# Part of w_out's rows moved from SyncE's queue to four-engine GpSimd loads, in a one-token decode kernel

## The chip, the cores and the metric

The kernel runs on one core of a Trainium2 chip. The metric is the device time in microseconds of one execution. Each time of a kernel is a median of several runs; a profile is one execution of its own, whose time is given beside its span.

## The reference

One token x (576 values) is normalized, and two branches are computed from it and added to it. Branch A is attention with a cache: 32 query heads, 16 key and value heads, of which the last 4096 positions are used. Branch B is a gated MLP with 2304 inner values.

```python
xn = layernorm(x)                                   # (1, 1, 576)
# A: attention over the last 4096 positions
q = (xn @ wq).reshape(32 heads, 128)
k, v = k_cache[:, :, -4096:], v_cache[:, :, -4096:] # 16 heads, each for two query heads
o = softmax(q @ k.T * 128 ** -0.5) @ v
A = o.reshape(4096) @ wo                            # wo: (4096, 576)
# B: gated MLP
z = gelu(xn @ w_in)                                 # w_in: (576, 4608)
z1, z2 = z[:2304], layernorm(z[2304:])
g = w_sp * z2 + b_sp                                # w_sp and b_sp are one value each
B = (z1 * g) @ w_out                                # w_out: (2304, 576)
out = x + A + B
```

Everything is bfloat16 in HBM. The two caches are 16.8 MB each as far as they are used, wq 4.7 MB, w_in 5.3 MB, wo 4.7 MB and w_out 2.7 MB.

## The kernel before

**Loads.** All large loads are issued by SyncE in the order of the list `order` (lines 103 to 104), w_out after it (line 117). They write tiles of one pool with eight buffers (`units`, line 60), so SyncE waits, before an issue, until PE has finished with the tile eight places before it. The order is wq (in parts), k0 to k3, v0, v1, two parts of w_in, and then k, v, the rest of w_in and wo in turn; the last ones are v6, v7, wo3 and w_out. Here k0 stands for the keys of two heads, 2 MB in 128 rows of 16 KB, one to a partition; v0 likewise. `wout_v` (line 78) puts 18 consecutive rows of w_out on each partition, and line 117 loads them in four pieces of 8, 6, 3 and 1 rows. ScalarE issues three tiny loads: x (line 71) and the two values w_sp and b_sp (lines 387, 388). GpSimd issues no load.

**Tables.** At the start GpSimd makes the identity and then `row_of` (lines 146 to 151), a table of 18 matrices of 128 x 128 ones and zeros. DVE makes small tables from the identity, among them `rem` and `col_of` (lines 152 to 153 and 209 to 216). With the two, `z_gate` (line 350) and `z_rows` (line 365) bring the gated values, which lie with the index 128 c + p, to the layout that w_out's rows have, 18 p + r: `z_gate` multiplies them into `spread`, and 18 matmuls with `row_of` as weights give `hp`, which DVE copies to `hv`, a column for each of a partition's 18 rows.

**Attention.** Blocks of the keys are transposed by eight matmuls (`T`, line 225) into PSUM, copied to a kT buffer by DVE or ScalarE (a pool of 20, `KTB`, line 35), and multiplied with q (`S`, line 237). The loop of line 404 runs over three rounds j = 1 to 3. In each, sixteen blocks of T run ahead of S by five, and of the products with v of the round before (`PV`, line 283) by seven. Between the rounds stand the softmax steps (`sm_max`, `sm_tr`, `sm_exp`, `sm_rec`), and the parts of the list in line 403: w_in's products (`z_part`), a permutation of the attention's output (`O_perm`) and the products with wo (`WO`). The gelu follows the third part of w_in; `z_gate` and `z_rows` are in round 3, at c = 1 and 8. PE's instructions run in the order in which they are written.

**The end.** After the last round come the PV of the last two pairs of heads (v6 and v7), `O_perm(3)`, `WO(3)`, and w_out's 18 rows (line 443). Each row is four matmuls of 144 columns, side by side in four column groups of the array (`out_mm`, line 305), all adding into one PSUM tile, `out_ps`. DVE copies it, and SyncE stores it.

## Time and profile before

| | |
|---|---|
| median of 3 runs | 130.89 us (130.76 to 131.17) |
| the profiled execution | 130.86 us, span 129.1 us |
| mean granted TensorE clock in it | 0.762 |
| bytes read | 50.96 MB, 395 GB/s over the span |
| PE, DVE, ScalarE, GpSimd busy | 72%, 45%, 22%, 6% of the span |
| w_out: first and last issue, last landing | 105.28, 110.72 and 125.69 us |
| PE's last matmul ends, the store is issued | 126.01, 126.40 us |

All times in the profile are microseconds from the start of the span. PE is TensorE, PEld its weight loads, DVE VectorE, ACT ScalarE, POOL GpSimd, SP SyncE; a q after a name means the engine's issuing side. In the chain of work, each line has its start, its length and what it was, a DMA from its issue to its landing; a timeline's lines have start, busy time, engine, line of the code, operation, output, inputs and shapes, and in brackets the idle time before it and what ended it. "Issue" stands there for a wait that no event in the profile explains. A digit in the rows of slices is the busy share of one fortieth of the span in tenths; q1 is SyncE's queue, q10 ScalarE's, and q8 the fetching of instructions.

### The profile page before, as it was taken

To read this page: it belongs to the slowest core of one execution; us is meant where nothing else is said; L and a number is where in the kernel's file an instruction comes from. 1 tells how busy PE (TensorE), PEld (TensorE's weight loads), DVE (VectorE), ACT (ScalarE), POOL (GpSimd) and SP (SyncE) were. 2 spreads that over 40 slices of the span, in tenths; PEclk is the share of its full clock that TensorE was granted. 3 is DMA by queue.
4 is the path that set the end of the run, shared out by engine and by line. 5 is a ranking of instruction groups with operands and counts; after the bars stand their busy time and mean duration, and the time that the engine had idled before them with its cause. 6 is when DMAs were issued, how large, how long until landed. Compare 5 with 4: busy or idle time off the path is not lost.

```text
span 129.1 us, 4567 instructions
## 1 busy us (share of the span) xinstructions
PE 93.1 (72%) x2135; PEld 86.9 (67%) x2135; DVE 57.8 (45%) x146; ACT 29.0 (22%) x34; POOL 7.1 (6%) x9
## 2 busy tenths in 40 slices
PE   3013999883986997927998959479549999587480
PEld 3013988773975997827988958468439998477460
DVE  6976768400564444305464524484823333430100
ACT  3001174500134353001363330105233330100000
POOL 7940000000000000000000000000000000000000
PEclk9999999965577699855599995558997555555559
DMA  4999999999999999999999999999999999999830
GB/s 117 436 398 444 436 426 402 448 431 416 416 431 431 413 428 416 439 416 436 411 431 421 424 396 449 416 436 421 426 426 411 415 433 431 419 407 416 358 135 0
DMA packets 4495, 51.23 MB, mean 397 GB/s; under 512 B 509, under 2 KB 638, under 8 KB 1022
## 3 DMA queue, kind: packets, MB, share of 16 engines
q1 hardware_dynamic: 4472, 50.96, 94.0%
q8 instruction: 16, 0.26, 0.8%
q14 instruction: 1, 0.01, 0.0%
q10 hardware_dynamic: 6, 0.00, 0.0%
HBM read 50.96 MB, written 0.00 MB: 395 GB/s over the span
## 4 chain that ended last, share of the span: by engine, by line
DMA 51%; PE 35%; issue 5%; DVE 4%; SPq 2%; ACT 1%
DMA v<-in_A_v_cache_dram 22%; DMA wq<-in_A_wq_dram 16%; PE tp L230 16%; DMA wout<-in_B_w_out_dram 13%; PE s L245 8%; PE o L289 5%; PE q_ps L377 2%; SPq L86 2%; PE zp L323 1%; DVE d L268 1%; DVE ss L273 1%; ACT p L270 1%; PE su L278 1%; PE s L242 1%; DVE mx L250 1%
## 5 line engine op out<-in xcount | busy, mean ns | idle before, releaser
L230 PE MATMUL tp<-ident,k 128*128 128x128 bf16 x512 | 44.5, 250 | 3.0 <-DVE kT L234 1.8
L230 PEld LDWEIGHTS <-k 128*128 128x128 bf16 x512 | 37.1, 114 | 4.2 <-issue 2.8
L234 DVE COPY kT<-tp 128x1024 bf16<-128x1024 bf16 x40 | 27.3, 690 | 24.5 <-PE tp L230 24.1
L232 ACT COPY kT<-tp 128x1024 bf16<-128x1024 bf16 x24 | 24.2, 1012 | 47.4 <-PE tp L230 47.4
L289 PE MATMUL o<-p,v 128*128 128x4 bf16 x512 | 19.8, 165 | 5.6 <-issue 2.9
L245 PE MATMUL s<-q_bf,kT 128*128 128x4 bf16 x512 | 20.9, 166 | 3.3 <-issue 3.3
L245 PEld LDWEIGHTS <-kT 128*128 128x128 bf16 x512 | 18.8, 102 | 4.3 <-issue 4.3
L289 PEld LDWEIGHTS <-v 128*128 128x128 bf16 x512 | 16.7, 100 | 6.3 <-issue 3.6
L250 DVE TENSOR_REDUCE mx<-s 128x8 f32<-128x512 f32 x4 | 2.8, 692 | 13.5 <-PE s L245 13.5
L270 ACT ACTIVATE p<-d 128x512 bf16<-128x512 f32 x4 | 2.5, 629 | 25.5 <-DVE d L268 25.5
L377 PEld LDWEIGHTS <-wq 128*128 128x128 bf16 x144 | 4.1, 101 | 2.7 <-issue 2.2
L377 PE MATMUL q_ps<-xe,wq 128*128 128x2 bf16 x144 | 4.0, 164 | 2.5 <-DVE xe L196 2.2
L278 PE MATMUL su<-ss,ones_f 128*128 128x8 f32 x8 | 2.2, 345 | 4.7 <-DVE ss L273 4.7
L278 PEld LDWEIGHTS su<-ss,ones_f 128*128 128x128 f32 x8 | 1.8, 279 | 5.2 <-DVE ss L273 5.2
L292 DVE TENSOR_TENSOR oTn<-o,rm 128x4 bf16<-128x4 f32 x8 | 1.3, 162 | 8.2 <-PE o L289 8.2
L307 PE MATMUL out_ps<-wo,oP 128*1 128x144 bf16 x128 | 4.5, 320 | 0.6 <-DVE oP L303 0.6
L323 PEld LDWEIGHTS <-win 128*128 128x128 bf16 x162 | 4.7, 104 | 0.1
L323 PE MATMUL zp<-xe,win 128*128 128x2 bf16 x162 | 4.8, 165 | 0.0
L168 PE MATMUL x_ps<-x,twice 64*128 64x9 bf16 x1 | 0.2, 164 | 5.3 <-DVE x L166 5.3
L273 DVE TENSOR_REDUCE ss<-p 128x8 f32<-128x512 bf16 x4 | 2.7, 686 | 2.8 <-ACT p L270 2.8
L264 PE MATMUL bc<-dg,ones_f 8*128 8x8 f32 x8 | 2.3, 360 | 2.3 <-issue 2.3
L307 PEld LDWEIGHTS <-oP 128*1 128x1 bf16 x128 | 3.3, 115 | 0.9 <-DVE oP L303 0.7
(94 smaller groups left out, 55.5 us busy)
## 6 DMA issues: line engine op xcount, KB each, us to landing
v<-in_A_v_cache_dram SPq DMA_DIRECT2D x8, 2048.0 KB, 27.3
k<-in_A_k_cache_dram SPq DMA_DIRECT2D x7, 2048.0 KB, 26.7
win<-in_B_w_in_dram SPq DMA_DIRECT2D x3, 1728.0 KB, 28.0
wo<-in_A_wo_dram SPq DMA_DIRECT2D x4, 1152.0 KB, 27.6
wq<-in_A_wq_dram SPq DMA_DIRECT2D x2, 2048.0 KB, 14.1
k<-in_A_k_cache_dram SPq DMA_DIRECT2D x2, 1024.0 KB, 11.1
wout<-in_B_w_out_dram SPq DMA_DIRECT2D x1, 1152.0 KB, 16.8
wout<-in_B_w_out_dram SPq DMA_DIRECT2D x1, 864.0 KB
```

Source lines behind the costliest of these rows:

```text
L230: nc.tensor.transpose(tp[:, i, :], kn[b][:, 8 * c + i, :], ident[:])
L232: nc.scalar.copy(kT[n][:], tp[:])
L234: nc.vector.tensor_copy(kT[n][:], tp[:])
L245: nc.tensor.matmul(s_ps[j][:, i, 8 * c + t, :], lhsT=kT[n][:, t, :], rhs=q_bf[:, 4 * b:4 * b + 4], start=False, stop=True, skip_group_chec ...
L250: nc.vector.tensor_reduce(out=mx[:], in_=s_ps[j][:].rearrange("p i t c -> p i c t"), axis=AXX, op=ALU.max)
L270: nc.scalar.activation(p[:], d[:], ACT.Exp, scale=SCALE)
L273: nc.vector.tensor_reduce(out=ss[:], in_=p[:].rearrange("p i t c -> p i c t"), axis=AXX, op=ALU.add)
L278: nc.tensor.matmul(su[:], lhsT=ones_f[:], rhs=sm[j]["ss"][:].rearrange("p i c -> p (i c)"), start=True, stop=True)
L289: nc.tensor.matmul(sm[j]["o"][:], lhsT=vn[b][:, t, :], rhs=p_sb[j][:, i, t, :], start=t == 0, stop=t == NT - 1)
L307: nc.tensor.matmul(out_ps[32 * g:32 * g + 1, :], lhsT=lhsT, rhs=rhs[:, OW * g:OW * (g + 1)], start=start, stop=last, tile_position=(0, 32 ...
L323: nc.tensor.matmul(zp[:, c, :], lhsT=win_t[r][:, P * c:P * (c + 1)], rhs=xe_of(r), start=(r == rows.start and c == 0), stop=r == rows.stop ...
L377: nc.tensor.matmul(q_ps[:, c, :], lhsT=wq_t[r][:, P * c:P * (c + 1)], rhs=xe_of(r), start=(r == 0 and c == 0), stop=r == NS - 1, skip_grou ...
```

## The change

w_out's first 1792 rows stay on SyncE's queue, 14 to a partition, in pieces of 7, 4, 2 and 1 rows. The other 512 go, eight to a partition, to 64 partitions: 16 to 31, 48 to 63, 80 to 95 and 112 to 127. They are a tile `wx` of their own, zero on the other partitions, and are loaded by four GpSimd DMAs of 16 partitions each (`load_wx`), in whose access pattern the source's outermost dimension has four elements and the destination's 16. Ahead of each stands a load of one value to each of four partitions of `junk4`. Two memsets on DVE, written after `z_part(2)` and `sm_rec(1)` at the end of round 1, touch `wx` and `junk4` first, so the loads wait for them. The eight rows of `wx` are multiplied between `WO(3)` and the rest of w_out, so the end has 22 rows of four matmuls. The tables follow the two layouts: `row_of` is made for 14 matrices of the first kind and four of the second, with more and smaller steps on GpSimd, which also sets `wx` to zero; `colA` and `colB` take the place of `col_of`, and `spreadB` stands beside `spread`. To make room, `KTB` goes from 20 to 16.

```diff
+RA = 14
+RB = 8
+FA = RA * P
+CB = FR - RA
-KTB = 20
+KTB = 16
...
-    wout_v = B_w_out.rearrange("(p r) n -> p r n", r=FR)
+    wout_v = B_w_out[0:FA].rearrange("(p r) n -> p r n", r=RA)
...
-    load_rows(wout_t, wout_v, "wout", D, (0, 8, 14, 17, 18))
+    load_rows(wout_t, wout_v, "wout", D, (0, 7, 11, 13, 14))
...
+    wx = const.tile([P, RB * D], BF16, name="wx")
+    wx_v = B_w_out[FA:FH].rearrange("(b s e r) n -> b e s (r n)", b=CB, s=4, r=RB)
+    junk4 = const.tile([4, 2], BF16, name="junk4")
...
-    nc.gpsimd.memset(row_of[:], 1.0)
-    nc.gpsimd.affine_select(out=row_of[:], in_=row_of[:], compare_op=ALU.is_ge, fill=0.0, base=0,
-                            pattern=[[P, FR], [-FR, P]], channel_multiplier=1)
+    nc.gpsimd.memset(row_of[:], 0.0)
+    nc.gpsimd.memset(row_of[:, 0:RA, :], 1.0)
+    nc.gpsimd.affine_select(out=row_of[:, 0:RA, :], in_=row_of[:, 0:RA, :], compare_op=ALU.is_ge, fill=0.0, base=0,
+                            pattern=[[P, RA], [-RA, P]], channel_multiplier=1)
...
+    for b in range(CB):
+        to = row_of[:, RA + b, 32 * b + 16:32 * b + 32].rearrange("m (e s) -> m e s", s=4)
+        nc.gpsimd.memset(to, 1.0)
+        nc.gpsimd.affine_select(out=to, in_=to, compare_op=ALU.is_ge, fill=0.0, base=0,
+                                pattern=[[-RB, 4], [-4 * RB, 4]], channel_multiplier=1)
+        nc.gpsimd.affine_select(out=to, in_=to, compare_op=ALU.is_ge, fill=0.0, base=RB - 1,
+                                pattern=[[RB, 4], [4 * RB, 4]], channel_multiplier=-1)
+    nc.gpsimd.memset(wx[:], 0.0)
...
-        spread = const.tile([P, FR, FR], BF16, name="spread")
-        nc.vector.tensor_tensor(out=spread[:], in0=col_of[:], in1=g[:].unsqueeze(2).to_broadcast([P, FR, FR]), op=ALU.mult)
-        return spread
+        spread = const.tile([P, RA, RA], BF16, name="spread")
+        nc.vector.tensor_tensor(out=spread[:], in0=colA[:], in1=g[:, 0:RA].unsqueeze(2).to_broadcast([P, RA, RA]), op=ALU.mult)
+        spreadB = const.tile([P, CB, RB], BF16, name="spreadB")
+        nc.vector.tensor_tensor(out=spreadB[:], in0=colB[:].unsqueeze(1).to_broadcast([P, CB, RB]),
+                                in1=g[:, RA:FR].unsqueeze(2).to_broadcast([P, CB, RB]), op=ALU.mult)
+        return spread, spreadB
...
+    def load_wx():
+        nc.vector.memset(wx[:, 0:1], 0.0)
+        nc.vector.memset(junk4[:], 0.0)
+        for b in (0, 2, 1, 3):
+            nc.gpsimd.dma_start(junk4[:, 0:1], B_w_out[FA:FA + 4, 0:1])
+            nc.gpsimd.dma_start(wx[32 * b + 16:32 * b + 32, :], wx_v[b])
...
+            if what == "z2":
+                load_wx()
...
-    for j in range(FR):
-        out_mm(hv[:, j:j + 1], wout_t[j], last=j == FR - 1)
+    for r in range(RB):
+        out_mm(hv[:, RA + r:RA + r + 1], wx[:, D * r:D * (r + 1)])
+    for j in range(RA):
+        out_mm(hv[:, j:j + 1], wout_t[j], last=j == RA - 1)
```

More of the change, by code (lines that the diff above doesn't have):

```diff
@@ L143 @@
     selr = const.tile([P, 8, 8, 16], BF16, name="selr")
+    wx = const.tile([P, RB * D], BF16, name="wx")
+    wx_v = B_w_out[FA:FH].rearrange("(b s e r) n -> b e s (r n)", b=CB, s=4, r=RB)
+    junk4 = const.tile([4, 2], BF16, name="junk4")
     row_of = const.tile([P, FR, P], BF16, name="row_of")
-    nc.gpsimd.memset(row_of[:], 1.0)
-    nc.gpsimd.affine_select(out=row_of[:], in_=row_of[:], compare_op=ALU.is_ge, fill=0.0, base=0,
-                            pattern=[[P, FR], [-FR, P]], channel_multiplier=1)
-    nc.gpsimd.affine_select(out=row_of[:], in_=row_of[:], compare_op=ALU.is_ge, fill=0.0, base=FR - 1,
-                            pattern=[[-P, FR], [FR, P]], channel_multiplier=-1)
-    rem = const.tile([P, 2, FR], FP32, name="rem")
-    col_of = const.tile([P, FR, FR], BF16, name="col_of")
+    nc.gpsimd.memset(row_of[:], 0.0)
+    nc.gpsimd.memset(row_of[:, 0:RA, :], 1.0)
+    nc.gpsimd.affine_select(out=row_of[:, 0:RA, :], in_=row_of[:, 0:RA, :], compare_op=ALU.is_ge, fill=0.0, base=0,
+                            pattern=[[P, RA], [-RA, P]], channel_multiplier=1)
+    nc.gpsimd.affine_select(out=row_of[:, 0:RA, :], in_=row_of[:, 0:RA, :], compare_op=ALU.is_ge, fill=0.0, base=RA - 1,
+                            pattern=[[-P, RA], [RA, P]], channel_multiplier=-1)
+    for b in range(CB):
[6 more added lines that the diff above has]
+    nc.gpsimd.memset(wx[:], 0.0)
+    remA = const.tile([P, 2, RA], FP32, name="remA")
+    colA = const.tile([P, RA, RA], BF16, name="colA")
+    colB = const.tile([P, RB], FP32, name="colB")
     out_ps = ps_c.tile([P, OW], FP32, name="out_ps")
@@ L208 @@
     nc.vector.tensor_copy(selr[:], ident[:].rearrange("p (q r) -> p r q", r=8).unsqueeze(2).to_broadcast([P, 8, 8, 16]))
-    whole = P // FR * FR
-    nc.vector.tensor_reduce(out=rem[:, 0, :], in_=ident_f[:, 0:whole].rearrange("p (q k) -> p k q", k=FR), axis=AXX, op=ALU.add)
-    nc.vector.tensor_add(rem[:, 0, 0:P - whole], rem[:, 0, 0:P - whole], ident_f[:, whole:P])
-    nc.vector.tensor_copy(rem[:, 1, :], rem[:, 0, :])
-    rem_r = rem[:].rearrange("p a k -> p (a k)")
-    for c in range(FR // 2):
-        nc.vector.tensor_copy(col_of[:].rearrange("p (b c) r -> p c b r", b=2)[:, c],
-                              rem_r[:, FR - 2 * c:2 * FR - 2 * c].unsqueeze(1).to_broadcast([P, 2, FR]))
+    whole = P // RA * RA
+    nc.vector.tensor_reduce(out=remA[:, 0, :], in_=ident_f[:, 0:whole].rearrange("p (q k) -> p k q", k=RA), axis=AXX, op=ALU.add)
+    nc.vector.tensor_add(remA[:, 0, 0:P - whole], remA[:, 0, 0:P - whole], ident_f[:, whole:P])
+    nc.vector.tensor_copy(remA[:, 1, :], remA[:, 0, :])
+    nc.vector.tensor_reduce(out=colB[:], in_=ident_f[:].rearrange("p (q k) -> p k q", k=RB), axis=AXX, op=ALU.add)
+    remA_r = remA[:].rearrange("p a k -> p (a k)")
+    for c in range(RA // 2):
+        nc.vector.tensor_copy(colA[:].rearrange("p (b c) r -> p c b r", b=2)[:, c],
+                              remA_r[:, RA - 2 * c:2 * RA - 2 * c].unsqueeze(1).to_broadcast([P, 2, RA]))
     kT, s_ps, p_sb, sm = {}, {}, {}, {}
@@ L312, in WO @@
             out_mm(oP[:, j, r:r + 1], wo_t[j][:, D * r:D * (r + 1)])
-    hv = const.tile([P, FR], BF16, name="hv")
+    hv = const.tile([P, RA + RB], BF16, name="hv")
     zacc = const.tile([P, FR, 2], FP32, name="zacc")
@@ L360, in z_gate, with z_rows @@
         nc.vector.tensor_mul(g[:], G[:, 0, :], gz[:])
-        spread = const.tile([P, FR, FR], BF16, name="spread")
-        nc.vector.tensor_tensor(out=spread[:], in0=col_of[:], in1=g[:].unsqueeze(2).to_broadcast([P, FR, FR]), op=ALU.mult)
-        return spread
-    def z_rows(spread):
-        hp = ps_m.tile([P, FR], FP32, name="hp", tag="m")
+        spread = const.tile([P, RA, RA], BF16, name="spread")
[4 more added lines that the diff above has]
+        return spread, spreadB
+    def z_rows(spread, spreadB):
+        hp = ps_m.tile([P, RA + RB], FP32, name="hp", tag="m")
         for c in range(FR):
-            nc.tensor.matmul(hp[:], lhsT=row_of[:, c, :], rhs=spread[:, c, :], start=c == 0, stop=c == FR - 1)
+            lo, hi, w = (0, RA, spread[:, c, :]) if c < RA else (RA, RA + RB, spreadB[:, c - RA, :])
+            nc.tensor.matmul(hp[:, lo:hi], lhsT=row_of[:, c, :], rhs=w, start=c in (0, RA), stop=c in (RA - 1, FR - 1))
         nc.vector.tensor_copy(hv[:], hp[:])
+    def load_wx():
[4 more added lines that the diff above has]
+            nc.gpsimd.dma_start(wx[32 * b + 16:32 * b + 32, :], wx_v[b])
     q_ps = ps_m.tile([P, 16, 2], FP32, name="q_ps", tag="m")
@@ L416 @@
             if j == 3 and c == 1:
-                spread = z_gate(G, sz)
+                spread, spreadB = z_gate(G, sz)
             if j == 3 and c == 8:
-                z_rows(spread)
+                z_rows(spread, spreadB)
             if c == ROUND + SLAG - 1:
```

## Prediction

> **What bounds the kernel now.** I read the shares of the engines first, then the chain that ended last in order of time, then PE's timeline of the last 35 us. From the page:

> ```profile
> PE 93.1 (72%) x2135; PEld 86.9 (67%) x2135; DVE 57.8 (45%) x146; ACT 29.0 (22%) x34; POOL 7.1 (6%) x9
> DMA  4999999999999999999999999999999999999830
> q1 hardware_dynamic: 4472, 50.96, 94.0%
> q8 instruction: 16, 0.26, 0.8%
> ```

> SyncE's queue (q1) keeps all sixteen DMA engines full until the last tenth of the span, so one expects the end to be set by bytes. The chain in order of time says where that is so:

> ```profile
> 67.50 28.78 DMA v<-in_A_v_cache_dram
> 96.33 0.35 PE o L289 x8
> ...
> 108.45 0.65 PE o L289 x24
> 109.12 16.20 DMA wout<-in_B_w_out_dram
> 125.36 0.69 PE out_ps L307 x16
> 126.07 0.31 DVE res L447
> ```

> The reader is to see two meetings of PE with the DMA engines: v4, issued at 67.50, lands at 96.28 and restarts PE at 96.33; and w_out's third piece restarts it at 125.36. Between them PE works or waits for itself:

> ```profile
> 96.33 0.35 PE L289 MATMUL o<-p,v 128*128 128x4 bf16 x8 [1.87 <-DMA v<-in_A_v_cache_dram]
> ...
> 120.31 0.38 PE L289 MATMUL o<-p,v 128*128 128x4 bf16 x8 [1.42 <-issue]
> 120.94 0.35 PE L298 MATMUL op<-oTn,selr 128*128 128x8 bf16 x8 [0.25 <-DVE oTn L292]
> 121.87 1.13 PE L307 MATMUL out_ps<-wo,oP 128*1 128x144 bf16 x32 [0.57 <-DVE oP L303]
> 122.78 1.18 PE L307 MATMUL out_ps<-wout,hv 128*1 128x144 bf16 x32
> 124.30 0.89 PE L307 MATMUL out_ps<-wout,hv 128*1 128x144 bf16 x24 [0.34 <-DMA wout<-in_B_w_out_dram]
> 125.36 0.65 PE L307 MATMUL out_ps<-wout,hv 128*1 128x144 bf16 x16 [0.17 <-DMA wout<-in_B_w_out_dram]
> ```

> From 122.78 the eighteen rows of w_out would need 18 x 0.12 us (the matmul groups of a row start 0.12 us apart here); the first group of the last row starts at 125.73 instead of 124.82, so waiting for w_out costs 0.91 us in all. That is the whole of what a faster w_out can give, however early it lands.

> The trace keeps sixteen landings of each load, one per DMA engine. They are even early (k1: 17.5 to 18.0, with one at 19.5) and split later: v4's come at 92.8 to 93.1 (seven), 93.7 (one), 94.4 to 94.7 (five) and 96.1 to 96.3 (three); w_out's last row lands at 122.3 to 123.1 (eight), 124.3 (one) and 125.4 to 125.7 (seven). The step is 1.5 us, and a new engine falls back just after each packet of q8. These packets (16 KB, 1.02 to 1.10 us, and the q1 packet beside them is stretched by about 0.5) fetch instructions: PE's long "issue" waits all lie at its 193rd instruction of a group of 256. So **eight engines carry the fetches**, in turn, and seven of them end some 3.1 us late; the other eight are early.

> **The change part by part.** Sum against the profiled run: 130.86 us, span 129.1, so 1.76 lies outside the span; the median is 130.89.

> w_out on q1: per engine eight packets each of 9216, 6912, 3456 and 1152 B become 8064, 4608, 2304 and 1152. The rows are 349, 265, 135 and 51 ns, so 6.40 us; interpolated between them, 307, 181, 93 and 51 ns, 5.06 us. Every engine is 1.34 us shorter, but only after wo3, behind everything else.

> The GpSimd loads carry 64 x 9216 B. On four engines each and eight engines in all, that is 8 packets of 9216 B, at 349 ns each: 2.79 us on each of eight engines. They start once DVE has passed the reciprocal at 61.53 (the new memsets follow it), and the tiny loads write one tile, so each waits for the one before; with waits in a full queue like that of ScalarE's two-byte loads (issued 23.2, landed 28.0) I estimate four rounds of 5 to 6 us, done by 85. So these 2.79 us stand **ahead of v4**, and the saving behind it. Bounds for the packet: 349 ns (the same size on q1) and, from the costliest foreign packet in the trace (the fetch's 1.57 us for 16384 B against 0.61), 2.6 times as much, 7.1 us an engine. I take 349, since it is the same copy from HBM to SBUF. The tiny loads are 9 ns packets, as ScalarE's were: below 0.2 us on any engine.

> So all depends on which engines they hit. On an early one, v4 lands at 93.1 + 2.8 = 95.9 (96.5 on the one at 93.7), beside 96.28: PE loses at most 0.2. On an engine that carries fetches it lands at 96.28 + 2.79 = 99.07, and all of PE's work from 96.33 starts 2.79 us later. What follows keeps up: v5, v6, v7 and wo3 land 2.79 later on that engine (101.2, 111.6, 116.6 and 119.3 before) and are met by a PE that is just as late.

> PE at the end: 22 rows instead of 18, the four extra 0.12 us each, but no waiting: if the eight rows of wx are there, the last row's first group starts at 122.78 + 21 x 0.12 = 125.30 instead of 125.73, 0.42 us sooner. w_out's last landing (125.7 now) would be 124.4 on a fetching engine without GpSimd load and 127.1 on one with it, where PE's last row comes at 128.1; so PE is the bound in either case.

> The instruction blocks: PE's extra 16 matmuls are 32 instructions, 4277 records become 4309. The boundaries met so far (705, 1473, 1729, 2497, 2753, 4033) make the next 4289, which PE does not reach now, but then does two rows before the end, at about 125.1. The sixteenth fetch begins at 123.67 and PE went on 2.4 to 2.6 us after the fetch in each of the six waits, so 126.2. But that fetch began the moment its engine's q1 was empty, and this is 1.34 us earlier then: 124.8. Cost 0 to 1.1 us; I take 0, by the emptier queue.

> POOL's start: memsets of 2304, 1792 and 4608 elements and two selects of 1792 by the rows 2.02 and 2.24 us per 2304, with twelve small ones at 0.1 to 0.29, make about 13 us where there were 6.5. DVE's casts beside them wait for POOL to end (the 128x128 cast took 2.01 us, to the end of POOL's memset), so xe, at 11.42 now, may be up to 4 us later. What hides it is PE's later waiting for DMAs, 0.77 at 67.5, 0.79 at 85.7 and 1.87 at 96.3; without that cover it would cost the 4 us, with it 0 to 0.6. I take 0. On POOL nothing is queued behind the loads; SyncE's order is unchanged.

> On DVE seven casts replace nine, one product becomes two of about 0.3 and 0.2 for 0.50; z_rows keeps 18 matmuls. Sixteen kT buffers are enough: the copy for a block waits for scores PE issued 11 blocks earlier. All 0; cover: the 1.87 us wait for v4.

> Sum for the likeliest case, at least one loaded engine also fetches: 130.86 + 2.79 - 0.42 = 133.2.

> **Which engines?** The trace does not number them. One row bears on it: the packets of ScalarE's queue (at 26.93 to 28.18) sit in the sequence of an engine that is among the three earliest in every later load, so that engine carries no fetch. If GpSimd's eight leave this one out, only seven early ones are left, and one fetching engine must take 2.79 us. Of the sets of eight, only one has no fetching engine.

> [...]

> **The rivals.** (1) Not slower: all eight loaded engines are early ones. Then v4 costs at most 0.2 and the end saves 0.42: 130.4 to 130.7, 130.6. For it: the early engines are eight, just as many, and their lead of 3.1 us is just over 2.79. It decides from the point where not one fetching engine is among the eight. (2) The same, but PE stands at its 4289th instruction until 126.2, with two rows to go: 0.6 later than now, 131.5. (3) The change doesn't do what it says: the loads spread over all sixteen engines, 4 x 349 ns = 1.40 on each; v4 is 1.40 later, the end 0.42 sooner, 131.8.

> **How the numbers follow.** Forecast 0.42 (133.2, its own range 132.7 to 134.2, since the waits for instructions move by half a microsecond and a GpSimd packet may cost more), (1) 0.34, (2) 0.12, (3) 0.12. About 0.3% (0.39 us) is what a measurement of this kernel can tell from no change. Of (1), 0.15 lies below 130.5 and 0.19 within; the rest is slower: 0.66. Cases of both signs hold the chance, so the range runs from 130.3 to 134.2 and leaves out some 0.1.

> **What would show it.** Right: v4's last landing near 99, PE's wait before it some 4 us where it is 1.87, no DMA wait before w_out's matmuls, and the digits of DMA thin out one slice later. Wrong: v4's landings close together near 96.3. An end of DMA before 125 with a PE that ends at 125.6 or later shows (1), an "issue" wait near 125 shows (2). A much later first q_ps matmul that still costs at the end would show the missing cover.

## The result, and the profile after

The changed kernel takes **137.53 us** (median of 6 runs, 136.44 to 137.9), the kernel before beside it on the same chip 130.99 us (6 runs, 130.76 to 131.21): a ratio of 1.0487, 95% interval 1.0448 to 1.0526. The forecast was slower, 133.2 us, with a range from 130.3 to 134.2. The sign came; the loss is 6.5 us where 2.3 were forecast. Where runs of one kernel below lie more than 1.5% apart (e1, e5 and e8), its ratio is that of the runs within 1.5% of its fastest. The profiled execution took 137.9 us, span 136.0, mean granted clock 0.761 (before 0.762).

From the page of the changed kernel, the lines that answer to those of before, and the row of bytes per slice (GB/s in each fortieth of the span, 3.4 us):

```profile
PE 95.1 (70%) x2151; PEld 89.7 (66%) x2151; DVE 61.8 (45%) x148; ACT 29.0 (21%) x34; POOL 18.5 (14%) x31
DMA  5999999999999999999999999999999999999610
GB/s 140 414 412 446 429 453 395 443 410 434 414 429 419 413 431 435 410 438 414 424 430 342 285 328 340 340 305 410 429 414 415 413 441 418 442 393 410 259 48 5
q1 hardware_dynamic: 4472, 50.37, 91.5%
q0 software_dynamic: 448, 0.59, 1.5%
q8 instruction: 17, 0.28, 0.8%
```

The row of bytes of the kernel before, in slices of 3.2 us:

```profile
GB/s 117 436 398 444 436 426 402 448 431 416 416 431 431 413 428 416 439 416 436 411 431 421 424 396 449 416 436 421 426 426 411 415 433 431 419 407 416 358 135 0
```

The busy digits of DMA are nines as before, and by them alone nothing has happened. The row of bytes shows it: from the 22nd to the 27th slice (71 to 92 us) the engines are as busy and move 285 to 342 GB/s where they move some 420 otherwise. The missing part is 610 GB/s x 3.4 us = 2.07 MB, 4.9 us at 425 GB/s. Queue q0, GpSimd's, appears with only 0.59 MB.

The four loads on it, in the timeline of GpSimd:

```profile
11.30 3.94 POOL L169 MEMSET wx<- 128x4608 bf16 x1
67.61 0.66 POOL L400 DMA_DIRECT2D junk<-in_B_w_out_dram  x1 [52.37 <-DVE om L321]
68.26 0.61 POOL L401 DMA_DIRECT2D wx<-in_B_w_out_dram  x1
73.39 0.53 POOL L400 DMA_DIRECT2D junk<-in_B_w_out_dram  x1 [4.51 <-DMA junk<-in_B_w_out_dram]
73.94 0.60 POOL L401 DMA_DIRECT2D wx<-in_B_w_out_dram  x1
79.92 0.53 POOL L400 DMA_DIRECT2D junk<-in_B_w_out_dram  x1 [5.38 <-DMA junk<-in_B_w_out_dram]
...
87.63 0.53 POOL L400 DMA_DIRECT2D junk<-in_B_w_out_dram  x1 [6.55 <-DMA junk<-in_B_w_out_dram]
```

The rounds are 5.8 to 7.7 us apart, as each tiny load waits for the one before. The packets tell the rest. A 16 KB packet of q1 takes 614 ns in this trace and one of 13.8 KB 520 ns. From 72.5 to 77.3, 79 to 82.9 and 86 to 90.6 us the first take 0.85 to 1.1 us and the second 0.70 to 0.86 (the first stretch), **on all sixteen engines**: in the middle of these stretches no such packet is below 1.3 times its usual time. And these are the times of the first three loads of wx (their packets run from 72.4, 78.9 and 85.7 us). Beside the fourth (93.0 to 97.0) the packets take 614 to 620 ns again. Three stretches of 13.3 us in all at 1.6 times the price lose some 5 us.

So v4 lands at 98.98 to 103.03 us where it was 92.76 to 96.28: the last engine 6.75 us later, and the first 6.2. PE's first q matmul in before, and PE's timeline in the changed kernel:

```profile
12.16 1.85 PE L377 MATMUL q_ps<-xe,wq 128*128 128x2 bf16 x64 [2.19 <-DVE xe L196]
```

```profile
16.04 1.85 PE L409 MATMUL q_ps<-xe,wq 128*128 128x2 bf16 x64 [5.73 <-DVE xe L215]
...
85.62 0.24 PE L309 MATMUL o<-p,v 128*128 128x4 bf16 x3 [3.22 <-issue]
...
93.74 0.27 PE L318 MATMUL op<-oTn,selr 128*128 128x8 bf16 x4 [3.51 <-issue]
...
103.24 0.34 PE L309 MATMUL o<-p,v 128*128 128x4 bf16 x8
...
129.17 1.13 PE L327 MATMUL out_ps<-wo,oP 128*1 128x144 bf16 x32 [0.57 <-DVE oP L323]
130.08 1.18 PE L327 MATMUL out_ps<-wx,hv 128*1 128x144 bf16 x32
131.04 1.73 PE L327 MATMUL out_ps<-wout,hv 128*1 128x144 bf16 x56
```

The reader is to see three things. PE's first q matmul is 3.88 us later (12.16 before): xe waited for GpSimd. PE meets v4 at 103.24, 6.91 later, and without a wait, since it is late itself: by its start, and by two waits for instructions of 3.22 and 3.51 us (1.48 and 1.62 in before). The slow queues may have made these two longer (in e1 below, without slow packets, they are 2.12 and 1.65 us); no run shows it. And from there to PE's last matmul (132.77) it is 29.53 us, 29.68 before: two differences cancel. In the 14.7 us after v4 the granted clock is 0.91 where it was 0.58, and the waits for instructions behind v4 come to 4.2 us where they were 1.4. The sum closes: 130.86 + 6.91 - 0.15, and 0.28 outside of PE's work, are 137.9. No wait for w_out is left at the end. The shares of the chain put this in one line each, before and after:

```profile
DMA 51%; PE 35%; issue 5%; DVE 4%; SPq 2%; ACT 1%
```

```profile
PE 62%; DVE 17%; issue 13%; ACT 5%; POOL 0%; POOLq 0%; ACTq 0%
```

A chain without DMA doesn't mean that DMA has no part. PE and v4 come within 0.2 us of each other, and the chain follows the one that came last; e2 below makes PE earlier and gains next to nothing.

### The profile page after: what moved, and what is told of

Its sections match the earlier page's. It is cut to its first block, busy times and chain, and to the rows that moved or that the text cites. A ratio compares the mean times of both kernels' runs of the same rounds, so it can differ in the third digit from the quotient of the medians.

```text
span 136.0 us, 4639 instructions
## 1 busy us (share of the span) xinstructions
PE 95.1 (70%) x2151; PEld 89.7 (66%) x2151; DVE 61.8 (45%) x148; ACT 29.0 (21%) x34; POOL 18.5 (14%) x31
## 3 DMA queue, kind: packets, MB, share of 16 engines
q1 hardware_dynamic: 4472, 50.37, 91.5%
HBM read 50.96 MB, written 0.00 MB: 375 GB/s over the span
## 4 chain that ended last, share of the span: by engine, by line
PE 62%; DVE 17%; issue 13%; ACT 5%; POOL 0%; POOLq 0%; ACTq 0%
PE tp L250 27%; PE s L265 10%; PE o L309 9%; PE out_ps L327 5%; ACT kT L252 3%; PE q_ps L409 3%; DVE rpar L209 3%; PE zp L343 2%; DVE mx L270 2%; DVE d L288 2%; DVE ss L293 2%; DVE other L145 2%; DVE ident_f L133 1%; PE su L298 1%; ACT p L290 1%
## 5 line engine op out<-in xcount | busy, mean ns | idle before, releaser
L250 PE MATMUL tp<-ident,k 128*128 128x128 bf16 x512 | 46.7, 259 | 2.9 <-DVE kT L254 1.5
L250 PEld LDWEIGHTS <-k 128*128 128x128 bf16 x512 | 39.6, 119 | 3.9 <-issue 3.8
L400 POOL DMA_DIRECT2D junk<-in_B_w_out_dram x4 | 2.2, 562 | 68.8 <-DVE om L321 52.4
L298 PE MATMUL su<-ss,ones_f 128*128 128x8 f32 x8 | 2.2, 342 | 4.5 <-DVE ss L293 4.5
L298 PEld LDWEIGHTS su<-ss,ones_f 128*128 128x128 f32 x8 | 1.8, 280 | 4.9 <-DVE ss L293 4.9
L318 PE MATMUL op<-oTn,selr 128*128 128x8 bf16 x32 | 1.6, 170 | 3.8 <-issue 3.5
L318 PEld LDWEIGHTS <-selr 128*128 128x128 bf16 x32 | 1.5, 111 | 4.0 <-issue 3.9
L209 DVE TENSOR_SCALAR rpar<-par,mv 128x2 f32<-128x2 f32 x1 | 3.8, 3757 | 0.6 <-ACT mv L204 0.6
## 6 DMA issues: line engine op xcount, KB each, us to landing
wq<-in_A_wq_dram SPq DMA_DIRECT2D x2, 2048.0 KB, 14.5
```

Of the source, the lines that this page charges most:

```text
L209: nc.vector.tensor_scalar_mul(rpar[:], par[:], mv[:, 3:4])
L250: nc.tensor.transpose(tp[:, i, :], kn[b][:, 8 * c + i, :], ident[:])
L298: nc.tensor.matmul(su[:], lhsT=ones_f[:], rhs=sm[j]["ss"][:].rearrange("p i c -> p (i c)"), start=True, stop=True)
```

## The experiments

**The theory and its rival.** Theory T, the forecast's: the loads run on eight engines, some of which fetch instructions, at 349 ns a packet. Theory N, a conjecture after the trace: each load of wx goes to the next four of the sixteen engines in turn, so that in the end all sixteen are used; each place in this turn has partitions of its own, and a load that writes others slows every engine. No trace shows which engine writes which partition, in these loads or in SyncE's; what the runs can show is at which place a load to which partitions is slow or free. A second rival is GpSimd's longer start. Medians of a few runs stand beside those of before (130.85 to 131.12 on each chip); the runs of e1, e5 and e8 scatter by 2.4 to 4.3 us, so their traces carry more than their times.

**e1: without the eight GpSimd loads; e5: with the tiny ones alone; e8: before, with GpSimd's longer start alone.**

```diff
 e1: -        for b in (0, 2, 1, 3):  (and both loads)
 e5: -            nc.gpsimd.dma_start(wx[32 * b + 16:32 * b + 32, :], wx_v[b])
 e8 (on before): -KTB = 20  +KTB = 16
 e8: +    wz = const.tile([P, 8 * D], BF16, name="wz")
 e8: +    nc.gpsimd.memset(wz[:, 0:2816], 0.0); nc.gpsimd.memset(wz[:], 0.0)
```

> The eight GpSimd loads are left out (wx stays zero, so 512 rows of w_out are missing from the result); everything else is the changed kernel. Theory L, the loads slow all sixteen DMA engines while they run (v4's last landing 103.0 instead of 96.3) and hold up the instruction fetches: v4 lands at 96.3 again; what is left is GpSimd's longer start, xe at 15.3 instead of 11.4, of which PE's waits absorb all but some 1.5 us, and 0.42 us less at the end: 131 to 132.5. Theory P, the late start of PE alone makes the loss: 137 stays.

> Only the four tiny loads are left, the four wx loads are out (512 rows of w_out are missing from the result). If GpSimd's loads as such (their descriptors and semaphore writes on all sixteen engines) slow the queue: packets above 0.8 us around each of them and a time over 133. If it is wx's own data: no slow packets, time that of the kernel without any GpSimd loads within 0.5 us.

> The kernel before, with KTB = 16 and with two more memsets on GpSimd after row_of (2816 and 4608 elements, some 6.4 us by its rate), so that GpSimd is busy to some 14.5 us as in the changed kernel; no GpSimd loads, w_out as before. If the late start of PE is absorbed by its later waits, as I forecast: within 0.6 us of before. By what the run without loads showed (PE reaches v4 3 us late, 133.1): 132.5 to 134.5, and KTB costs nothing.

e1: ratio 1.0004 (0.996 to 1.0048; ten runs, 130.40 to 133.92 us). v4 lands at 96.25 and w_out's last row at 124.37, where before had 96.28 and 125.69. So q1's part is 1.32 us shorter and v4 is on time: all of v4's lateness comes from the GpSimd loads. SyncE's later issue of v4 is no rival: it stands at 73.55 us in the changed kernel and at 67.50 in before, but at 72.92 in e1 too. e5: ratio 1.0052 (1.0017 to 1.0087; seven runs, 131.12 to 133.5), no slow packets, v4 at 96.33: not from the tiny ones.

PE meets v4 at 97.09 in e5 and at 97.47 in e8, where it was 96.33; in e1's profile, an execution of 133.72 us, at 99.30. So GpSimd's longer start makes PE later at this point, by 0.8 us in e5 and 1.1 in e8, as soon as v4 doesn't cover it. Of this little is left at the end of those two profiles (PE's last matmul ends at 126.10 in e5 and 126.27 in e8, 126.01 in before), and e8's fastest run, 131.35 us, is 0.2 us above before on its chip. Its other three runs take up to 135.68; what makes some runs of these three kernels 2 to 4 us longer, nothing here shows. How much of PE's lateness is the start and how much the waits for instructions, which move with it, these runs don't separate.

**e2: wx set to zero later**, in eight pieces from 34.22 us on.

```diff
-    nc.gpsimd.memset(wx[:], 0.0)
...
+    nc.vector.memset(wx[:, 0:1], 0.0)
+    for i in range(8):
+        nc.gpsimd.memset(wx[:, D * i:D * (i + 1)], 0.0)
```

> wx is set to zero by GpSimd at about 33 us, in eight pieces, instead of in one memset of 3.9 us at 11.3. Theory L: xe is back near 11.8, PE starts 3.5 us sooner, but v4 still lands near 103, so the end hardly moves: 136 to 137.5. Theory P: 133 to 134.

137.26 us (136.96 to 137.5), ratio 1.0484 (1.0467 to 1.0501). The first q matmul is back at 12.49 and PE waits for v4, which lands at 102.93:

```profile
102.98 0.35 PE L308 MATMUL o<-p,v 128*128 128x4 bf16 x8 [2.55 <-DMA v<-in_A_v_cache_dram]
```

In the changed kernel the start is covered by v4; the loads set the time.

**e3: without the tiny loads; e6: each wx load ahead of its tiny one; e4: the loads in the order 3, 1, 2, 0; e7: other rows of w_out on the same partitions.**

```diff
 e3: -            nc.gpsimd.dma_start(junk4[:, 0:1], B_w_out[FA:FA + 4, 0:1])
 e6: the same line behind the load of wx
 e4: -        for b in (0, 2, 1, 3):
 e4: +        for b in (3, 1, 2, 0):
 e7: -            nc.gpsimd.dma_start(wx[32 * b + 16:32 * b + 32, :], wx_v[b])
 e7: +            nc.gpsimd.dma_start(wx[32 * b + 16:32 * b + 32, :], wx_v[b ^ 1])
```

> The four tiny loads are out, the wx loads stay. New theory N: the tiny loads do not move GpSimd's choice of engines, so the four wx loads go one after the other over all sixteen engines, four at a time (which is why no engine falls behind the others), and a load slows everyone when its four engines write partitions that are not those they write in SyncE's loads; only the last load meets its own. N: the last load (b = 3) is free, the three before it are slow, 136 to 138, as in the changed kernel. Theory S, the tiny loads do move it and the slowing has another cause: another pattern of slow and free loads, or a lag between the engines that grows by about 1.4 us.

> Each wx load stands ahead of its tiny load, so that by a cursor that moves four engines at a time the wx loads fall on the four engines that the tiny loads had, and the other way round. If the loss lies in which engines get the bytes (my forecast's reason: engines that also fetch instructions), the time moves by more than 1.5 us, and the lag of the last landings behind the first, 4.0 us at v4 now, changes by some 2.8. If the slowing of all sixteen engines is what costs, the time stays within 1.5 us of 137.4 as long as the packets beside the loads are slow again.

> The four wx loads in the order b = 3, 1, 2, 0 instead of 0, 2, 1, 3. In the changed kernel the q1 packets of all engines take 0.9 to 1.0 us instead of 0.61 while the first three wx loads run, and 0.61 beside the fourth (b = 3). If the slowing belongs to the rows read or the partitions written: full rate beside the first load, slow beside the other three, same total within 1 us. If it belongs to the place in the order or the time: slow beside the first three again, the fourth free, time within 0.7 us.

> Each wx load reads the rows of its neighbour (b exchanged 0 with 1, 2 with 3), so the result is not the reference's; partitions written, engines and order are those of the changed kernel. There the load for partitions 112 to 127 (fourth, b = 3) leaves the other packets alone, and with the order reversed it was b = 1 in second place. If the rows read decide: the second load (now rows of b = 3) is free and the fourth (rows of b = 2) slows the others. If the partitions written decide: the fourth is free again.

e3 took 136.26 us (two runs; ratio 1.0407, 1.0362 to 1.0452), e6 136.68 (136.38 to 138.0), e7 136.71 (one run): in all three the first three loads have slow packets beside them and the fourth none, as in the changed kernel. Hence the tiny loads change nothing in what the loads of wx hit; and the rows that are read don't matter. In e3 and e4 PE starts as late as in the changed kernel and still waits 1.86 and 2.82 us for v4, so there too the loads set the time. e4 took 137.43 (136.61 to 137.82), and there the *second* load is the free one. So it depends on the place in the sequence together with the partitions written: last with 112 to 127, or second with 48 to 63.

**e9: loads of wx with 16 as the outermost dimension; e11: one load at each place of the turn, on partitions that theory N takes for that place's own.** In e9 the pattern's outermost dimension is 16 on both sides, which was meant to spread each load over all sixteen engines; its loads have 32 packets each on q0, those of e3 80. In e11 the loads go to the partitions 0, 16, 64 and 80 onward, in this order, and by theory N all four of them are free.

```diff
 e9:  -rearrange("(b s e r) n -> b e s (r n)", b=CB, s=4, r=RB)
 e9:  +rearrange("(b q r) n -> b q (r n)", b=CB, r=RB)   (and no tiny loads)
 e11: +BASE = (0, 16, 64, 80)
 e11: -        for b in (0, 2, 1, 3):
 e11: +        for b in (0, 1, 2, 3):
 e11: -            nc.gpsimd.dma_start(wx[32 * b + 16:32 * b + 32, :], wx_v[b])
 e11: +            nc.gpsimd.dma_start(wx[BASE[b]:BASE[b] + 16, :], wx_v[b])
```

> The same four wx loads by GpSimd at the same place, but with 16 as the outermost dimension on both sides, so that each is spread over all sixteen engines (one partition each, 349 ns by the size); tiny loads out, tables fitted. If four engines' concentrated bytes make the slowing: no packets above 0.8 us, v4 at 97.7 (1.40 later), PE's late start decides: 132.5 to 134. If any GpSimd load of this size does: slow packets again and 136 to 138.

> The changed kernel with the wx rows on partitions 0 to 15, 16 to 31, 64 to 79 and 80 to 95, loaded in this order, tables fitted. [...] S: slow packets again, 136 to 138.

The rows of bytes per slice, of e9 and of e11:

```profile
GB/s 135 429 407 446 429 433 406 432 433 414 433 409 426 427 414 444 400 443 414 424 385 173 196 232 413 437 409 433 419 429 428 396 439 423 429 405 415 316 83 5
```

```profile
GB/s 111 441 398 449 436 411 410 452 416 431 426 416 424 420 419 427 428 431 411 431 426 411 410 420 423 439 409 424 418 431 410 420 439 426 412 409 411 286 61 0
```

In e9 the rate falls to 173 GB/s (packets of 1.2 to 1.76 us), v4 lands at 104.05, and the time is 137.14 us (136.63 to 137.94). In e11, with as many bytes from the same queue, there is no dip: v4 lands at 97.94, 1.66 later than before where the loads' own packets are 4 x 349 ns = 1.40, and the time is 132.96 us (132.61 to 134.32), ratio 1.0184 (1.012 to 1.0248). This is the experiment that decides for N: the partitions alone take 5.1 of v4's 6.75 us away. The spread of v4's landings is 3.4 us (3.5 in before), so each engine has got about the same.

The trace numbers no engine; what supports theory N is its hits. Let A to D be the four places in GpSimd's turn, A that of the first load. The partitions at which a load of that place was free in these runs are called its own: A 0 to 15 and 32 to 47, B 16 to 31 and 48 to 63, C 64 to 79 and 96 to 111, D 80 to 95 and 112 to 127. The changed kernel, e3, e6 and e7 send A to 16, B to 80, C to 48 (slow) and D to 112 (own: free); e4 A to 112 (slow), B to 48 (own: free), C to 80 and D to 16 (slow); e11 all to their own. The runs below add 28 more loads to own partitions, all free. That the place and the partitions together decide is shown; why they do is not.

**e12: tiny loads in the form of wx's; e13: the same with wx set to zero late.** If a tiny load covers 16 partitions with an outermost dimension of four, it should, by theory N, take its turn of four engines, and wx meets B, D, B, D, on eight engines, as the change means it.

```diff
 e12: -    junk4 = const.tile([4, 2], BF16, name="junk4")
 e12: +    junk4 = const.tile([16, 2], BF16, name="junk4")
 e12: -            nc.gpsimd.dma_start(junk4[:, 0:1], B_w_out[FA:FA + 4, 0:1])
 e12: +            nc.gpsimd.dma_start(junk4[:, 0:1], wx_v[0][:, :, 0:1])
 e13: e12 with the edit of e2
```

> The tiny loads get the form of the wx loads (16 partitions, four as the source's outermost dimension, one value each), everything else is the changed kernel. [...] If the form does not matter: as the changed kernel, 137.

> The same with wx set to zero late, in eight pieces at about 33 us. N, with the eight loaded engines the early ones: v4 near 96.5, PE on time, the end 0.4 us sooner than before: 130.3 to 131.2. N with fetching engines among them: 133 to 133.6, the sum of my forecast. If the slowing stays: 137.

No slow packets in either. e12: 134.34 us (133.28 to 134.72), ratio 1.0248 (1.0199 to 1.0296). e13: 133.87 us (132.89 to 134.31), ratio 1.0214 (1.0164 to 1.0264), v4 at 99.57 (forecast 99.07). In e12 it lands at 97.81, though the loads hit the same engines: by the landings, none of the loaded engines that fetch has carried two fetches by then, where three have in e13 (99.34 to 99.57; two others land at 97.68 and 97.86). PE's timeline of e13 at v4:

```profile
99.62 0.36 PE L308 MATMUL o<-p,v 128*128 128x4 bf16 x8 [2.08 <-DMA v<-in_A_v_cache_dram]
```

w_out's last row lands in e13 in four groups: 121.2 to 122.4 (five engines), 123.9 to 124.7 (six), 125.9 (one) and 127.4 to 127.6 (four). The four last ones are fetching engines with GpSimd's packets on top (124.4 without by e1, 127.1 with by the forecast), and so is the one at 125.9, with one fetch less: e1 has one such engine at 122.85. So this is the forecast's kernel and its number: theory T was right of a kernel whose tiny loads move the turn, and the changed kernel isn't that.

**e16: e11 with wx set to zero late** (the edit of e2).

> e11 (one wx load on each four engines, on their own partitions, spread over all sixteen) with wx set to zero late, in eight pieces. v4 lands 1.4 to 1.7 later than before, at 97.7 to 97.9, and with xe in time PE meets it within 0.1: 131.8 to 132.5, where e11 took 132.96; the difference to e11 is the price of GpSimd's longer start. If the start costs nothing once the slow packets are gone, the time is e11's, 132.9.

132.68 us (131.96 to 133.26), ratio 1.0132 (1.0102 to 1.0162); v4 at 97.98, PE there at 98.02. The start's price beside a late v4 is 0.3 us here and 0.5 between e12 and e13, within the runs' spread.

**e14, e15, e17, e18: which engines fetch.** All have wx's zeros late and loads to own partitions only; None is a small load in wx's form, which moves the turn by one place (e12 and e13: wx behind such loads is free at B, D, B, D).

```diff
 e14: BASE = (0, 16, 32, 48)     for b in (0, 1, None, None, 2, 3, None, None):    A, B, A, B
 e15: BASE = (64, 80, 96, 112)   for b in (None, None, 0, 1, None, None, 2, 3):    C, D, C, D
 e17: eight partitions a load on two engines of B and two of D, 16 on A            A, half B, half D, twice
 e18: RA = 16; BASE = (0, 32)    for b in (0, None, None, None, 1):                A, A; half the rows
```

> The change, with small loads in wx's own form (16 partitions) in place of the one-value loads, so that they count in GpSimd's turn over the engines: wx in the first and second, fifth and sixth place, on the first eight engines, and on the partitions 0 to 63; wx is set to zero late, in eight pieces, as in e13. No load leaves its engines' own partitions, so no slow packets. If the engines that fetch instructions are the last eight, this reaches what the change was after: the early engines take 2.79 us, v4 lands at 96.0 to 96.6, the spread of its landings falls from 3.5 to 1 us, w_out's last landing is near 124.4, and the end saves some 0.4: 130.2 to 131.2. If four of the first eight fetch, as of the eight in e13, v4 lands near 99.1 to 99.6 and the time is 133 to 134.

> As e14, with wx on the last eight engines and the partitions 64 to 127. If those are the ones that fetch instructions, all eight of them take the 2.79 us: v4 lands at 99.1 to 99.6, its landings are spread by 6 us, w_out's last row lands late on all eight of them near 127.2, and the time is 133 to 134. If four of them fetch, the same time with four late landings of w_out. If none does: 130.2 to 131.2.

> The counts of loaded engines that also fetch instructions, read from w_out's last landings (four of the fifth to eighth and last four in e12, two of the first eight in e14, six of the last eight in e15, and two among the fifth to eighth by the landings between e12's first two loads) leave the first four without any, the ninth to twelfth all fetching, and two in each of the other groups. If the fetching ones lie in a row, they are the seventh to fourteenth in GpSimd's count. This kernel is e14 with wx on the other eight: loads of four engines on the first four, and of two on the fifth and sixth and on the last two, all on their own partitions. If that is right, v4 lands at 95.8 to 96.6 with a spread of 1 us where before had 3.5, w_out's last row lands at 124.1 to 124.6 on all engines, and the time is 130.2 to 131.2, near the rival's 130.6: no fetching engine among the eight. If the two of a group are not those, two or four fetching engines are hit: v4 near 99.2 and 133.3 to 134.3. If loads of two engines don't move the turn by two, the landings show another count.

> e14 with 16 rows to a partition on SyncE's queue and only 256 rows on GpSimd's, two loads of 16 partitions, both on the first four engines, the only group without a fetching engine by the landings so far (e13 after its first load, on the fifth to eighth: two late engines of 3.2 to 3.4 us; e16 after its first, on the first four: none). Three small loads stand between the two. If the fetching engines alone set v4's landing, the same 2.79 us an engine cost nothing here: v4 lands at 96.2 to 96.6, its spread stays 3.5 us, w_out's last row lands near 125.0, and the time is 130.5 to 131.3, that of before. If GpSimd's loads cost by something else, v4 lands at 97.5 or later and the time is over 132.

| | median us (range) | ratio (95%) | v4's last landing | loaded engines that also fetch |
|---|---|---|---|---|
| e14 | 133.56 (132.64 to 134.3) | 1.0191 (1.0158 to 1.0223) | 99.25 | 2 of 8 |
| e15 | 134.47 (134.43 to 134.77) | 1.0279 (1.0264 to 1.0294) | 99.40 | 6 of 8 |
| e17 | 133.12 (132.9 to 134.7) | 1.0193 (1.015 to 1.0236) | 97.93 | 2 of 8 |
| e18 | 131.79 (131.36 to 132.34) | 1.0075 (1.0051 to 1.0099) | 96.84 | 0 of 4 |

The last column counts w_out's landings that carry both delays: in e14 and e17 two each (127.3 and 127.4), in e15 six (five from 127.2 to 127.5 and one, with one fetch less, at 126.1). Counted so, e12 and e13 have five on B and D, not the four that the expectations of e14 and e17 took. No loaded engine of A is among them (e18: w_out's last landing is 125.50). So of the eight fetching engines A has none, B two, C three and D three. e17 was to avoid them all by a guess at the pairs in B and D, and the guess, which rested on the wrong count (C four, D two), failed: two of its loaded engines fetch. There one load ran behind v4, so v5 shows the whole delay (104.50, 101.19 in before). e18 loads A alone, with half the rows, and 2.79 us an engine as in the forecast. PE at v4 there:

```profile
96.89 0.35 PE L309 MATMUL o<-p,v 128*128 128x4 bf16 x8 [1.13 <-DMA v<-in_A_v_cache_dram]
```

v4 is 0.56 late, not 2.97 to 3.29 (e13 to e15): the same 2.79 us an engine, on four engines that don't fetch, cost a fifth. The 0.56 was expected to be 0.3 at most; one early engine has always been 0.6 to 0.9 behind its fellows (93.69 in before), and with 2.79 more it is the last. e18 remains 0.9 us slower than before, some 0.35 us more than v4's lateness, for a reason that was not found. It is the fastest of all the versions that load w_out from GpSimd; none beats before. A version on all eight early engines would have to split pairs, and wasn't tried.

## Why the prediction was wrong

**The step that failed** is the second term, "the GpSimd loads carry 64 x 9216 B. On four engines each and eight engines in all ... 2.79 us on each of eight engines". Rival (3) had the engines right (all sixteen, 1.40 us each) and the price wrong. Its price in v4's landing is 6.75 us: 1.66 for the even spread (e11) and 5.1 for what three of the four loads do to the packets of all others. The bound taken for a packet on q0 (2.6 times 349 ns, 7.1 us an engine) looked at the packet of the load, which took some 505 ns in the slow rounds, while the price falls on the packets of q1 beside it. The fetch's row, a q1 packet stretched by 0.5 us beside it, showed that kind of price, and was used for one engine only.

**The engines.** The text left open which engines GpSimd's loads hit and drew two cases from it, early or fetching. It took for granted that the tiny loads take their turn. e3, e6 and e12 show that those in the change's form don't: without them (e3) and with them behind the loads of wx (e6) the same three loads are slow and the fourth is free, and with tiny loads in wx's form (e12) none is slow. Why a tiny load in the change's form doesn't move the turn, no trace shows.

**The mechanism** stood for the kernels that the forecast describes: a fetching engine that takes 2.79 us more brings v4 to 99.07 by the forecast and to 99.25, 99.40 and 99.57 in e14, e15 and e13, with medians of 133.56, 134.47 and 133.87 where 133.2 was forecast. It holds for an engine that has carried two fetches by then; in e12, where none of the loaded ones had, v4 landed at 97.81. With no fetching engine hit, e18's v4 comes at 96.84, near the forecast's 96.5 for "the one at 93.7". Rival (1) would have needed all eight early ones; the eight that the change means (B and D) hold five that fetch.

**q1's 1.34 us**: 1.32 in e1 (the 4608 B packet, taken as 181 ns, is 178 by interpolation and 179.5 in the changed kernel's trace, which makes the term 1.36 or 1.37). **The end**: in e13, whose clock (0.54) and waits for instructions (1.3 us) behind v4 are like those of before (1.4 us), it is 29.27 us from v4 to PE's end, 29.68 before: 0.41 saved, 0.42 forecast, from one profile of each. In the changed kernel the clock and longer waits for instructions lie over it (29.53); PE waits for no w_out there either. **The 4289th instruction**: no wait there in the changed kernel; the 17th fetch begins at 132.7, when PE is done. Taken 0, and it is.

**GpSimd's start** (cost taken 0, bound 0.6): its size was right (wx is zero at 15.24 us, xe 4 us later), its cover was not the one named. The three waits, 3.43 us, would leave 0.45 of xe's 3.88; with v4 on time PE comes 0.8 us late to it in e5, and 1.1 in e8, whose start is 3.23 us later and would be covered. What it costs at the end stays open: 0.2 us by e8's fastest run, 0.5 and 1.1 by the ratios of e1 and e5 if the 0.42 of the end is added. In the changed kernel it costs little (137.53 against e2's 137.26), because v4 is later still. **KTB, DVE's casts, the tiny loads' bytes**: nothing visible (e13 and e16, with sixteen buffers, meet v4 within 0.05 us).

**The range** ended at 134.2, though the bound of 7.1 us an engine, kept in the text, would have given 137.5. It should have been in the range.

## What to carry to other kernels

When a DMA writes a few partitions by a few engines, find by experiment which partitions it can write at which place in the sequence of such loads, and judge by the duration of the *other* queue's packets: here the wrong partitions cost 5.1 us (e11 against the changed kernel) and the bytes themselves 1.4 to 1.7. A row of nines in DMA's busy digits hides this; the row of GB/s below it doesn't. Before bytes are moved between engines, find by experiment which engines each load hits, since a load that is meant only to shift the turn may not shift it (e3, e6).

## What the runs showed of the hardware

```profile
L209 DVE TENSOR_SCALAR rpar<-par,mv 128x2 f32<-128x2 f32 x1 | 3.8, 3757 | 0.6 <-ACT mv L204 0.6
```

```profile
11.49 0.23 DVE L208 TENSOR_SCALAR rpar<-par,mv 128x2 f32<-128x2 f32 x1 [0.60 <-ACT mv L203]
```

The first line is the changed kernel, where the operation ends at 15.27 us and GpSimd's memset at 15.24; the second is e2, where no memset stands beside it and it takes 0.23 us. That such operations stand beside GpSimd's was in the forecast.
